# A planner that holds large transfers back while others fill the DMA queue, with q and k loaded per pair of heads and a new order table

## The chip, the cores and the metric

The program runs on one core of a Trainium2 chip, in one launch. The metric is device time in microseconds, the median of several runs. TensorE (PE, its weight loads PEld) multiplies; VectorE (DVE), ScalarE (ACT) and GpSimd (POOL) do the rest; SyncE (SP) only issues DMAs, all of them here, in a single queue that it works through in order.

## The reference, cut to what matters

Three stages follow each other, all in float32. (1) Attention: 4 batches, 12 heads, 448 rows, head width 64; q and k are normalized by their root mean square and scaled by a gain, then softmax(q k^T / 8) v. (2) A mixture of 4 causal attention experts on the 768-wide result: each row's two best experts, by `x @ w_gate`, are added with softmax weights. (3) A causal 5-tap convolution over rows makes a sigmoid gate, which multiplies `x @ w_val`; the product goes through `w_out`.

```
q_n, k_n = rmsnorm(q, g_q), rmsnorm(k, g_k)
x   = softmax(q_n k_n^T / 8) v                      # 4 x 12 heads
x   = sum over the 2 chosen experts e of  w_e * (softmax_causal(x wq_e (x wk_e)^T / 8) x wv_e) wo_e
out = (sigmoid(conv5(x)) * (x w_val)) w_out
```

## The kernel before, in words

Attention works on 24 pairs of heads (`pair`, n = 0 to 23). `normed` runs for every second pair: it loads q and k of four heads into one of two `raw` buffers (tiles w; lines 588 to 596), squares them on ACT (L601), sums on DVE (L605), gets the root by Ln and Exp (L614, L615) and a few small DVE steps (L619), and scales q and k into tiles s (L631, on POOL, on DVE for the first two pairs). For the first two pairs alone the load is already cut per pair, into one buffer each. `pair` then transposes on PE (L669), splits each value into a high and a low fp32r part (tiles qd, ql, xa), and needs copies of some halves on other partitions: those are small DMAs of 112 KB from on-chip memory to on-chip memory, two in `duplicate` (L559, L560) and two in `interleave` (L572, L573), where the second waits until the first has landed. They gate the score matmuls (L731). Row maximum (DVE L735), exp (ACT L736), transposes (PE L754), splits (L336, L759), and the products with v (L763, L765) follow; `row_factors` sends the reciprocal row sums through memory (L528, L530). Every sixth pair, `project` multiplies a finished batch with the expert weights (L789, L792). After the last pair the experts (`experts`, L958 to L1016), the fused output weights and the gate (`gated`, L1050 to L1085) and the output product (`project_out`, L1107, stores at L1116 to L1120) follow, batch by batch. `out_weights` brings `w_out` in twelve blocks through one buffer, rawb: load (L468), decoding on DVE (L474 to L476, L482), store (L853), reload (L855), split (L336, L331).

The order of the instructions of every engine is not written by hand. Each step is recorded by `op` with an engine, a planned duration, a priority vt (smaller is earlier; from the table `VT` and the step's place in its loop), a planned latency lat, and for a large DMA xfer, the time it occupies the DMA queue in the plan. `Plan.order` then plays the steps through: whenever an engine is free, it takes, of the steps whose inputs and buffers are there, the one of smallest vt, and so writes the order of each engine. `passed` is the planned time at which the DMA queue has emptied; a transfer begun now adds to it (line 231: `passed = max(now + ISSUE, passed) + pick.xfer`, ISSUE 500 ns) and is planned to land accordingly later. The chip has only the order: each engine runs its list in order, and an instruction waits there for what it needs.

On SP the priorities are, from first to last, in the table before: q and k loads (vt -1273 and on, `(n0 - VT["nl"]) * 12.6`), the gain loads `load_g` (-1247; four DMAs, planned as one step of 2500 ns without xfer), the row factors (-394 and on), `w_val` blocks, the on-chip copies (1421 and on), expert weights (2480 and on), v (7128 and on), and stores of the projections last.

Of the kernel before, what the change touches and what calls it, by code (L numbers as in the profile page):

```python
# [22 lines left out]


ISSUE = 500

# [22 lines left out]
def c_ptt(n):  # L49
# [8 lines left out]


VT = {  # L60
# [8 lines left out]
    "d_ph": 12.553, "d_pl": 32.0444, "d_ux": 525.5817, "d_ua": 647.7012, "d_um": 427.5213, "d_dup": 643.6909, "d_sc": 35.8393, "d_vh": 0.568, "d_vl":  # L69
    0.0, "d_kh": 122.0232, "d_ah": 141.9673, "d_xh": 355.494, "d_xl": 194.8804, "d_pv": 84.2769, "d_x2": 449.3647, "d_out": 580.9012, "d_oh":  # L70
    176.1229, "d_ol": 508.4987, "d_wh": 101.5984, "d_wl": 352.2573, "d_th": 19.0436, "d_tl": 137.7431, "d_v2h": 1061.6258, "d_v2l": 218.3702, "d_fh":
    674.3617, "d_fl": 711.8051, "d_qh": 577.4214, "d_ql": 60.1478, "d_evh": 721.7186, "d_evl": 349.74, "d_eah": 74.7536, "d_eal": 780.7673, "d_yh":
    629.5812, "d_yl": 391.7836, "d_gh": 461.9232, "d_tiny": 7.3052, "d_gl": 759.8279,
}


# [33 lines left out]
class Plan:  # L110
# [53 lines left out]
    def order(self):  # L164
        engs = ("pe", "act", "dve", "pool", "sp", "host")
        free_at = dict.fromkeys(engs, 0.0)
        queue = {e: [] for e in engs}
        events = []
        done = []

        def push(o):
            for x in o.alts:
                heapq.heappush(queue[x[0]], (o.vt, o.seq, o, x))
                if x[3] > 0.0:
                    heapq.heappush(events, (o.ready + 1000.0 * x[3], 2, o.seq, o))

        for o in self.ops:
            if o.npred == 0:
                push(o)
        now, ports, passed = 0.0, 0.0, 0.0  # L180
        left = len(self.ops)

        def can(o):
            need = {}
            for b in o.bufs:
                if b.kind is not None and b.phys is None:
                    g = self.groups[b.group]
                    if not b.kind.open or b.seq != g[2] + need.get(b.group, 0) or g[3] + need.get(b.group, 0) >= g[0]:
                        return False
                    need[b.group] = need.get(b.group, 0) + 1  # L190
                    need[b.kind] = need.get(b.kind, 0) + 1
                    if need[b.kind] > len(b.kind.free):
                        return False
            return True

        while left:
            progress = True
            while progress:
                progress = False
                for e in engs:  # L200
                    if free_at[e] > now:
                        continue
                    skipped, pick, choice = [], None, None
                    while queue[e]:
                        item = heapq.heappop(queue[e])
                        if item[2].begun:
                            continue
                        held = ports > now and item[2].port.get(e, False)
                        if not held and item[2].ready + 1000.0 * item[3][3] <= now and can(item[2]):
                            pick, choice = item[2], item[3]  # L210
                            break
                        skipped.append(item)
                    for item in skipped:
                        heapq.heappush(queue[e], item)
                    if pick is None:
                        continue
                    for b in pick.bufs:
                        if b.kind is not None and b.phys is None:
                            g = self.groups[b.group]
                            b.phys = b.kind.free.pop(0)  # L220
                            g[2] += 1
                            g[3] += 1
                    pick.begun = True
                    pick.eng, pick.dur, pick.fn, _ = choice
                    if pick.lat is None:
                        pick.lat = LAT[pick.eng]
                    free_at[e] = now + pick.dur
                    if pick.port.get(e, False):
                        ports = free_at[e]
                    if pick.xfer:  # L230
                        passed = max(now + ISSUE, passed) + pick.xfer
                        pick.lat += max(passed - free_at[e], 0.0)
                    pick.end = now + pick.dur
                    heapq.heappush(events, (pick.end, 0, pick.seq, pick))
                    heapq.heappush(events, (pick.end + pick.lat, 1, pick.seq, pick))
                    done.append(pick)
                    left -= 1
                    progress = True
            if not events:
                stuck = [(o.vt, o.eng, [(b.group, b.seq) for b in o.bufs if b.kind and b.phys is None]) for e in engs for _, _, o, _ in queue[e]]  # L240
                raise RuntimeError(f"the plan is stuck with {left} operations: {sorted(stuck)[:20]}")
            now = events[0][0]
            while events and events[0][0] <= now:
                _, what, _, o = heapq.heappop(events)
                if what == 2:
                    continue

                for s in o.succ:
                    if (len(s.alts) == 1 and s.eng == o.eng and o.eng in ("pe", "act")) == (what == 0):
                        s.npred -= 1  # L250
                        if s.npred == 0:
                            s.ready = now
                            push(s)
                if what == 0:
                    continue
                for b in o.bufs:
                    b.uses -= 1
                    if b.uses == 0 and b.kind is not None:
                        b.kind.free.append(b.phys)
                        self.groups[b.group][3] -= 1  # L260
                if o.eng == "host":
                    for kind in o.opens:
                        kind.open = True
        self.makespan = now
        return done
# [3 lines left out]
def tile_attn_moe_gate(  # L269
# [17 lines left out]
    nc = tc.nc  # L287
# [5 lines left out]
    T = 112  # L293
    NT = S // T
# [13 lines left out]
    op, buf = plan.op, plan.buf  # L308
# [50 lines left out]
    cw = cpool.tile([P, NCH, KC], F32, name="cw")  # L359
# [144 lines left out]
    TP = 12.6  # L504
# [70 lines left out]
    def normed(n0):  # L575

        b, p = divmod(n0, NPAIR)
        sqs = []
        for m0, nm in ((0, 1), (1, 1)) if n0 == 0 else ((0, 2),):
# [5 lines left out]
            def halves(raw=raw, nm=nm):  # L585
                return raw.t[0:T, 0 : 1024 * nm].rearrange("p (i m s t d) -> p i m s t d", i=2, m=nm, s=2, t=NT)

            for i, src in enumerate((q, k)):

                def load(i=i, src=src, raw=raw, m0=m0, nm=nm):  # L590
                    o = raw.t[0:T, 0 : 1024 * nm].rearrange("p (i h e) -> p i h e", i=2, h=2 * nm)[:, i]
                    h = 2 * (p + m0)
                    nc.sync.dma_start(o, src[b, h : h + 2 * nm].rearrange("h (p t) d -> p h (t d)", t=NT))

                op("sp", 450, load, (n0 - VT["nl"]) * TP - 2.0 * (n0 == 0), w=[raw], lat=1700, xfer=900 * nm)
            for m in range(nm):
                sq = buf(kS, "sq", QUOTA["sq"])
                sqs.append(sq)
# [17 lines left out]
            t = buf(kM, "t", 2)  # L616
# [551 lines left out]
```

## Time and profile before

| | us |
|---|---|
| median of 3 runs (642.06 to 643.44) | 642.58 |
| the profiled execution's own time | 643.4 |
| its span, first to last instruction | 641.6 |
| PE busy | 591.3 (92%) |
| PEld busy | 540.5 (84%) |
| DVE busy | 517.7 (81%) |
| ACT busy | 476.1 (74%) |
| POOL busy | 395.9 (62%) |

Of the span 1.8 us lie outside the profile's first and last instruction (643.4 less 641.6), and the profiled execution is 0.8 us above the median of the runs. Busy time is what an engine's instructions cover; DMA-issuing instructions are not counted. The clock column is the granted TensorE clock as a share of its full level (2.4 GHz; the lower level is 1.2 GHz); its mean over the span is 0.987.

### The profile page before, as it was taken

How to read it: one execution, taken by the hardware profiler on the slowest of the kernel's cores; microseconds unless marked ns; L12 is line 12 of the kernel's file. 1: busy time of each engine (PE TensorE's matmuls, PEld its weight loads, DVE VectorE, ACT ScalarE, POOL GpSimd, SP SyncE). 2: the span in 40 equal slices, each digit the busy share in tenths (PEclk: the TensorE clock that was granted, in tenths of full speed). 3: DMA queues.
4: the chain of work that ended last, by engine and by line, in shares of the span. 5: the costliest groups of instructions: out<-in, count | busy, mean ns of one | idle time of the engine just before them, and what ended most of it. 6: DMA issues, size and time to landing. Idle time of an engine off the chain costs nothing.

```text
span 641.6 us, 11699 instructions
## 1 busy us (share of the span) xinstructions
PE 591.3 (92%) x3626; PEld 540.5 (84%) x3626; DVE 517.7 (81%) x1013; ACT 476.1 (74%) x1189; POOL 395.9 (62%) x568
## 2 busy tenths in 40 slices
PE   1697799999999999999999999999869999999997
PEld 0575689888988988988989899989669999999997
DVE  5899899899999989999998938899987765973800
ACT  4798788789988988989886747777795677583431
POOL 4469775676758685958572467788887296216050
PEclk9899999999999999999999999999879999999999
DMA  6627751584273753543335387747343233100111
GB/s 172 139 49 165 147 129 42 154 191 144 56 179 90 181 138 100 145 128 101 90 96 170 105 252 221 207 156 240 107 135 116 75 93 89 39 26 32 46 49 64
DMA packets 70658, 77.93 MB, mean 121 GB/s; under 512 B 23442, under 2 KB 66618, under 8 KB 70596
## 3 DMA queue, kind: packets, MB, share of 16 engines
q1 hardware_dynamic: 70596, 77.18, 44.3%
q8 instruction: 29, 0.48, 0.3%
q14 instruction: 33, 0.27, 0.1%
HBM read 47.52 MB, written 15.87 MB: 99 GB/s over the span
## 4 chain that ended last, share of the span: by engine, by line
PE 53%; DVE 19%; DMA 10%; ACT 9%; POOL 4%; issue 3%; SPq 1%; ACTq 0%; DVEq 0%; POOLq 0%
PE bank L1107 12%; PE bank L789 6%; PE bank L731 6%; PE bank L754 6%; DVE x L759 4%; PE bank L1077 3%; PE bank L763 3%; DMA qd<-qd 3%; PE bank L792 3%; DVE m L735 3%; PE bank L1050 3%; ACT f L736 2%; PE bank L765 2%; ACT x L336 2%; PE bank L1008 2%
## 5 line engine op out<-in xcount | busy, mean ns | idle before, releaser
L336 ACT ACTIVATE x<-bank 128x448 fp32r<-128x448 f32 (+6 forms) x260 | 122.9, 505 | 21.5 <-PE bank L1008 10.4
L736 ACT ACTIVATE f<-bank,m 128x448 f32<-128x448 f32 x168 | 106.3, 633 | 23.4 <-DVE m L735 19.9
L759 DVE TENSOR_TENSOR x<-bank,x 128x448 fp32r<-128x448 f32 x192 | 114.9, 615 | 7.1 <-ACT x L336 4.6
L754 PE MATMUL bank<-ident,f 128*128 128x128 f32 (+1 forms) x768 | 111.6, 279 | 6.1 <-ACT f L736 5.8
L754 PEld LDWEIGHTS bank<-ident,f 128*128 128x128 f32 (+1 forms) x768 | 101.2, 176 | 15.7 <-ACT f L736 7.0
L735 DVE TENSOR_REDUCE m<-bank 128x1 f32<-128x448 f32 x168 | 103.0, 614 | 6.1 <-PE bank L731 5.0
L763 PE MATMUL bank<-x,ra 128*128 128x448 f32 x192 | 78.3, 409 | 5.5 <-DVE x L759 3.9
L731 PE MATMUL bank<-xa,qd 128*128 128x448 f32 x192 | 72.1, 396 | 11.6 <-DVE xa L697 5.5
L1107 PE MATMUL bank<-wp,rb 128*128 128x384 f32 x308 | 73.0, 341 | 0.3 <-POOL rb L331 0.3
L789 PE MATMUL bank<-x,wp 128*128 128x448 f32 x288 | 72.7, 378 | 0.0
L1058 DVE SCALAR_TENSOR_TENSOR f<-bank,cw,f 128x445 f32<-128x445 f32 (+3 forms) x96 | 59.5, 673 | 9.4 <-ACT f L1054 9.1
L731 PE MATMUL bank<-xa,ql 128*128 128x448 f32 x168 | 62.9, 375 | 0.0
L331 POOL TENSOR_TENSOR f<-f,f 128x448 f32<-128x448 f32 x32 | 37.3, 1166 | 30.6 <-DVE f L540 8.7
L631 POOL TENSOR_TENSOR s<-w,m 112x512 f32<-112x512 f32 x46 | 48.2, 1071 | 12.7 <-DVE m L619 11.0
L765 PE MATMUL bank<-x,ra 128*128 128x448 f32 x144 | 54.5, 379 | 1.3 <-DVE x L759 1.2
L1107 PEld LDWEIGHTS bank<-wp,rb 128*128 128x128 f32 x308 | 54.6, 188 | 1.1 <-POOL rb L331 0.6
L789 PEld LDWEIGHTS bank<-x,wp 128*128 128x128 f32 x288 | 50.9, 189 | 3.5 <-ACT f L736 0.2
L731 PEld LDWEIGHTS bank<-xa,qd 128*128 128x128 f32 x192 | 36.7, 194 | 17.1 <-POOL ra L331 5.8
L1107 PE MATMUL bank<-wp,ra 128*128 128x384 f32 x196 | 50.9, 343 | 0.0
L540 DVE TENSOR_TENSOR f<-bank,f 64x448 f32<-64x448 f32 x64 | 39.6, 619 | 10.9 <-ACT f L336 8.9
L763 PEld LDWEIGHTS bank<-x,ra 128*128 128x128 f32 x192 | 36.5, 190 | 13.3 <-DVE x L759 8.4
L792 PE MATMUL bank<-wp,x 128*112 128x260 f32 x288 | 44.4, 291 | 0.0
(170 smaller groups left out, 1426.1 us busy)
## 6 DMA issues: line engine op xcount, KB each, us to landing
f<-rr_d SPq DMA_DIRECT2D x64, 112.0 KB
xa<-xa SPq DMA_DIRECT2D x59, 112.0 KB
qd<-qd SPq DMA_DIRECT2D x46, 112.0 KB
w<-in_q_dram SPq DMA_DIRECT2D x11, 448.0 KB
w<-in_k_dram SPq DMA_DIRECT2D x11, 448.0 KB
s<-in_v_dram SPq DMA_DIRECT2D x12, 384.0 KB
s<-in_moe_w_val_dram SPq DMA_DIRECT2D x12, 384.0 KB
rawb<-in_moe_w_out_dram SPq DMA_DIRECT2D x12, 384.0 KB
```

What stands on the lines that cost most here:

```text
L336: either(kinds, dvt, n, act=lambda: nc.scalar.activation(out(), a(), AF.Copy), vec=lambda e: e.tensor_scalar(out(), f32(a()), 1.0, 1.0, op ...
L731: nc.tensor.matmul(sc.t[:, 0:S], l, r, start=(m == 0), stop=(m == len(ops) - 1))
L735: op("dve", c_dve(S), lambda i=i, sc=sc: nc.vector.tensor_reduce(nm.t[:, i : i + 1], sc.t[:, 0:S], axis=AX.X, op=ALU.max, negate=True), vt ...
L736: op("act", c_act(S, 2), lambda i=i, sc=sc: nc.scalar.activation(a[i].t, sc.t[:, 0:S], AF.Exp, bias=nm.t[:, i : i + 1], accum_out=sm.t[:, ...
L754: nc.tensor.transpose(at.t[0:cn, P * i : P * (i + 1)], a[3 * s + i].t[:, cols], ident)
L759: op("dve", c_dve(S), lambda at=at, hi=hi, lo=lo, cn=cn, r0=r0, own=own: nc.vector.tensor_tensor(lo.t[r0 : r0 + cn], at.t[0:cn, own], hi.t ...
L763: nc.tensor.matmul(acc.t[:, 0:S], l, hi.t, start=(j == 0), stop=(j == 3))
L765: nc.tensor.matmul(acc.t[:, 0:S], l, lo.t, start=False, stop=False)
L789: nc.tensor.matmul(acc.t[:, 0:S], wp[:, w, c, m * P : (m + 1) * P], x.t, start=first, stop=last)
L792: nc.tensor.matmul(acc.t[0:T, 0:VC], x.t[:, t * T : (t + 1) * T], wp[:, w, c, 2 * ED : WC], start=first, stop=last)
L1058: nc.vector.scalar_tensor_tensor(gc.t[:, d:S], acc.t[:, 0 : S - d], cw[:, c, KC - 1 - d : KC - d], gc.t[:, d:S], op0=ALU.mult, op1=ALU.add)
L1107: nc.tensor.matmul(acc.t[:, 0:NH], l.t[:, cols], wout[:, w, c, NH * h : NH * (h + 1)], start=(c == 0 and i == 0), stop=(c == NCH - 1 and i ...
```

## The change

A transfer of xfer 600 or more is not begun by the plan while the planned queue reaches more than 1000 ns ahead of now; when it has drained to that point, an event lets SP look again. The loads of q and k are cut into one per pair of heads and tensor (224 KB, xfer 1050) also for the blocks after the first. And all priorities have new values. The rest of the kernel, its buffers and its arithmetic are as before.

```diff
+HOLD, BIG = 1000, 600
 VT = {
-    "pw": 197.4989, "nl": 101.0747, ...  "vl": -565.7674, "tr": -112.8122, ... "lg": -1246.9721, ...
+    "pw": 223.8855, "nl": 297.1005, ...  "vl": -797.0996, "tr": -109.5638, ... "lg": -1785.5091, ...
     ...
-                        held = ports > now and item[2].port.get(e, False)
+                        held = ports > now and item[2].port.get(e, False) or item[2].xfer >= BIG and passed > now + HOLD
     ...
                     if pick.xfer:
                         passed = max(now + ISSUE, passed) + pick.xfer
                         pick.lat += max(passed - free_at[e], 0.0)
+                        heapq.heappush(events, (passed - HOLD, 2, pick.seq, pick))
     ...
-            for i, src in enumerate((q, k)):
-                def load(i=i, src=src, raw=raw, m0=m0, nm=nm):
-                    o = raw.t[0:T, 0 : 1024 * nm].rearrange("p (i h e) -> p i h e", i=2, h=2 * nm)[:, i]
-                    h = 2 * (p + m0)
-                    nc.sync.dma_start(o, src[b, h : h + 2 * nm].rearrange("h (p t) d -> p h (t d)", t=NT))
-                op("sp", 450, load, (n0 - VT["nl"]) * TP - 2.0 * (n0 == 0), w=[raw], lat=1700, xfer=900 * nm)
+            for m in range(nm):
+                for i, src in enumerate((q, k)):
+                    def load(i=i, src=src, raw=raw, m0=m0, nm=nm, m=m):
+                        o = raw.t[0:T, 0 : 1024 * nm].rearrange("p (i h e) -> p i h e", i=2, h=2 * nm)[:, i, 2 * m : 2 * m + 2]
+                        h = 2 * (p + m0 + m)
+                        nc.sync.dma_start(o, src[b, h : h + 2].rearrange("h (p t) d -> p h (t d)", t=NT))
+                    op("sp", 450, load, (n0 - VT["nl"]) * TP - 2.0 * (n0 == 0), w=[raw], lat=1700, xfer=1050)
```

In the new table the order of the classes on SP is the same: q and k (-3743 and on), the gain loads (-1785), row factors (-881 and on), the first `w_val` block, the on-chip copies (1380 and on), expert weights (2813 and on), v (10043 and on).

## Rows read from the trace of the kernel before

**Rows 1.** Windows: span in stages; busy of each engine, clock, DMA share, GB/s.
```profile
core 0: us, PE busy (x) PEld busy (x) DVE busy (x) ACT busy (x) POOL busy (x), PEclk, DMA share, GB/s
0.00:10.00 10.00, 0.00 (x0) 0.00 (x0) 3.80 (x10) 4.83 (x8) 3.90 (x23) 1.00 0.62 164
40.00:85.00 45.00, 37.00 (x208) 29.91 (x209) 39.04 (x68) 37.19 (x90) 38.95 (x51) 0.96 0.58 124
100.00:340.00 240.00, 232.70 (x1490) 210.81 (x1490) 226.80 (x421) 210.34 (x521) 166.46 (x232) 1.00 0.47 124
450.00:480.00 30.00, 22.24 (x116) 19.45 (x115) 25.36 (x58) 23.78 (x61) 24.39 (x34) 0.83 0.43 123
500.00:641.60 141.60, 137.57 (x821) 132.32 (x820) 74.72 (x161) 75.85 (x186) 51.39 (x82) 1.00 0.18 55
```

**Rows 2.** Waits of PE over the whole span: us in total, times, longest.
```profile
PE bank L669 <- DVE m L619: 10.5, 1, 10.5
PE bank L1008 <- DVE f L1085: 4.8, 1, 4.8
...
PE bank L731 <- DMA qd<-qd: 2.7, 3, 1.8
...
PE bank L731 <- DMA xa<-xa: 1.2, 2, 0.7
```

**Rows 3.** Chain that ended last, between 55 and 79 us: start, us, what.
```profile
55.82 7.53 DMA qd<-qd
...
63.44 2.12 DMA qd<-qd
...
70.31 6.31 DMA qd<-qd
76.70 2.17 DMA qd<-qd
```

**Rows 4.** SP's issues: copies behind q and k loads, and one without.
```profile
54.23 0.43 SPq L593 DMA_DIRECT2D w<-in_q_dram  x1
54.76 0.43 SPq L593 DMA_DIRECT2D w<-in_k_dram  x1
...
55.82 0.48 SPq L559 DMA_DIRECT2D qd<-qd  x1
...
63.44 0.48 SPq L560 DMA_DIRECT2D qd<-qd  x1
...
330.58 0.48 SPq L559 DMA_DIRECT2D qd<-qd  x1
...
333.11 0.47 SPq L560 DMA_DIRECT2D qd<-qd  x1
```

**Rows 5.** Waits of SP's queue over the whole span: us in total, times, longest.
```profile
SPq L560 <- DMA qd<-qd: 34.6, 13, 4.8
```

**Rows 6.** Timeline of the start: issues of SP and the first steps behind them.
```profile
1.17 0.45 SPq L593 DMA_DIRECT2D w<-in_k_dram  x1
2.66 0.58 SPq L447 DMA_DIRECT2D g<-in_g_q_dram  x1
4.55 0.60 SPq L448 DMA_DIRECT2D g<-in_g_k_dram  x1
4.62 1.06 ACT L601 ACTIVATE s<-w 112x1024 f32<-112x1024 f32 x1 [2.62 <-DMA w<-in_k_dram]
7.46 0.21 DVE L452 TENSOR_SCALAR gg<-g 128x1 f32<-128x1 f32 x1 [0.53 <-DMA g<-in_g_k_dram]
7.69 1.22 DVE L605 TENSOR_REDUCE m<-s 112x16 f32<-112x1024 f32 x1
8.83 0.88 DVE L619 SCALAR_TENSOR_TENSOR m<-m,m 112x16 f32<-112x16 f32 x4
```

**Rows 7.** Windows within the start of attention, same columns as rows 1.
```profile
55.00:60.00 5.00, 3.04 (x19) 2.18 (x17) 5.00 (x9) 4.44 (x12) 4.66 (x7) 1.00 0.98 219
75.00:80.00 5.00, 2.78 (x11) 2.00 (x12) 2.94 (x6) 3.65 (x10) 4.42 (x6) 0.90 0.79 146
80.00:85.00 5.00, 5.00 (x26) 4.45 (x25) 4.34 (x7) 3.82 (x10) 4.75 (x7) 0.76 0.33 76
```

**Rows 8.** Who waits for the q and k loads, over the whole span.
```profile
  DMA w<-in_k_dram: 4.9, 4
```

**Rows 9.** SP's issues of rawb: the last four of twelve loads.
```profile
441.13 0.38 SPq L468 DMA_DIRECT2D rawb<-in_moe_w_out_dram  x1
463.42 0.33 SPq L468 DMA_DIRECT2D rawb<-in_moe_w_out_dram  x1
469.76 0.37 SPq L468 DMA_DIRECT2D rawb<-in_moe_w_out_dram  x1
481.70 0.34 SPq L468 DMA_DIRECT2D rawb<-in_moe_w_out_dram  x1
```

More of the change, by code (lines that the diff above doesn't have):

```diff
@@ L60 @@
 VT = {
[8 rows of a table removed]
[L69 to L73, printed above, removed]
[8 rows of a table added]
+    "d_ph": 67.3095, "d_pl": 232.558, "d_ux": 559.7588, "d_ua": 561.4908, "d_um": 271.0272, "d_dup": 479.8107, "d_sc": 20.7623, "d_vh": 1.0708,
+    "d_vl": 0.0, "d_kh": 120.8591, "d_ah": 376.0376, "d_xh": 412.9286, "d_xl": 84.9786, "d_pv": 128.2464, "d_x2": 670.1971, "d_out": 188.3538, "d_oh":
+    354.9454, "d_ol": 340.6525, "d_wh": 26.7103, "d_wl": 274.7178, "d_th": 187.244, "d_tl": 187.6038, "d_v2h": 1073.4642, "d_v2l": 843.0787, "d_fh":
+    834.5908, "d_fl": 830.1554, "d_qh": 690.35, "d_ql": 157.8726, "d_evh": 759.1297, "d_evl": 398.9279, "d_eah": 557.6893, "d_eal": 1050.2794, "d_yh":
+    115.3421, "d_yl": 268.7796, "d_gh": 210.8442, "d_tiny": 4.6612, "d_gl": 816.7842,
 }
```

16 rows, old and new, of the table VT are left out of this document.

## The prediction

> **What bounds the kernel now.** I read the stage windows first, then the waits of PE, then the chain, and last SP's issues. In the windows [rows 1] the reader is to see three kinds of stretches. From 500 us to the end PE is busy 137.57 of 141.6 us: that stretch is PE's, and no transfer can give it much. From 100 to 340 us PE is busy 232.7 of 240 (3.0% idle) and DVE 226.8 (5.5% idle): two engines are nearly full. The room lies in three places: the start, where PE waits 10.5 us for its first input [rows 2]; 40 to 85 us, where PE idles 8.0 of 45 us and DVE 6.0; and 450 to 480 us, where PE idles 7.8 of 30 and the clock that it is granted is 0.83 [rows 1].
>
> PE's waits on the small on-chip copies, the transfers that the new rule is to let through, are 2.7 + 1.2 = 3.9 us in all [rows 2]. The chain says more than that sum: between 55.8 and 79 us it runs over these copies for 7.53 + 2.12 + 6.31 + 2.17 = 18.1 us [rows 3]. SP's issues show why [rows 4]. At 54.23 and 54.76 it issues 448 KB of q and of k, right behind them the first copy at 55.82, and the second, which waits until the first has landed, goes out at 63.44: 7.6 us later. Where no such load is ahead, the same step takes 2.5 us (330.58 to 333.11). So a block's loads cost a copy about 5.1 us. SP, which works in order, stood 34.6 us in 13 such waits [rows 5], yet PE waited for it only 3 times. In most blocks the delay is hidden behind work on other pairs.
>
> **The change: the start, +1.1 us.** The new rule can be played through in the code for the first steps. The plan's times (ns) only give an order here. At 0 SP takes the first q load; `passed` becomes 500 + 1050 = 1550. At 450 SP is free, and k is next by priority, but 1550 > 450 + 1000, so it is held, by 100 ns. The gain loads have no xfer, cannot be held and come next in priority: one step of four DMAs, 2500 ns. So the first k goes out fifth from there, not second, and k of the second pair after two more small transfers. On the chip a gain issue takes 0.58 to 0.60 us [rows 6]; four of them with the gaps are from 2.66 to 4.55 + 0.60, that is 2.5 us. The first k is issued at 1.17 and lets the square begin at 4.62 [rows 6]; I expect its issue near 3.7 and the square near 7.0 (a little less than 2.5 later, since fewer bytes are in the queue). Two things are given back: the wait of DVE for the gains, 0.53 us, goes, since they land earlier; and the sum of the second pair (7.69, 1.22 us) no longer stands in front of the first pair's small steps, which begin at 8.83 and could have begun about 0.8 earlier [rows 6]. So 2.4 - 0.5 - 0.8 = +1.1. Bounds: -0.5, if the square is no later and only the gain wait goes, and +2.5, if nothing is given back. PE has no other work then, and DVE is busy from there on, so all of it reaches the end.
>
> **The copies, -4.6 us.** Between 40 and 85 us a copy that finds at most one load of 224 KB ahead should take some 3 us rather than 7.6. PE's direct waits there and the clock that falls behind the longest one (0.90 and 0.76 in 75 to 85 us [rows 7]) would give 2.8 us of the 3.9 and 0.1 x 2.8 + 0.24 x 5.0 = 1.5 us. But DVE sets how much can be had: it idles 6.0 us of the 45, and at the 5.5% of the following stretch it would idle 2.5. In 55 to 60 us it is busy all 5.0 us while the copy is outstanding [rows 7]. So I take the excess, 3.5 us. In the rest of attention the direct waits left are 3.9 - 2.8 = 1.1 us, and I take them all: -4.6 in sum. Bounds: 0 (DVE's list fills the time anyway) and -8.0, all of PE's idle time in the 45 us.
>
> **The split of q and k, 0.** 22 loads of 448 KB become 44 of 224 KB, 22 issues more of some 0.47 us [rows 4], 10.3 us of SP in 300. Cover: loads run a block ahead into the second raw buffer, and in the whole span only 4 squares waited for one, 4.9 us, most of it at the start [rows 6, 8]. If that cover is gone, the price is in the fourth rival. What is queued behind a load that waits for its raw buffer is every later transfer on SP, copies too; the four loads of a block wait for the same buffer, so this head is not longer than before.
>
> The Trainium skill speaks against the split: "DMA: Bandwidth & Descriptors", section Rules for kernel authors, asks for one large transfer in place of many small ones. The windows lean its way so far: 164 GB/s at the start, where q and k come in loads of 224 KB [rows 1], against 219 GB/s where they are 448 KB [rows 7]; but other small transfers lie in both.
>
> **The new table, 0.** The order of the classes on SP is unchanged (read from the diff), so the rule and the split decide what changes there. What else moves in the lists can't be read from rows. The place with most at stake is 450 to 480 us. There PE idles 7.8 us, 4.8 of it in one wait [rows 2], and at clock 0.83 the 22.2 busy us hold 3.8 us of loss: 11.5 us at most to gain. `w_out` passes through one buffer in twelve loads, the last four at 441, 463, 470 and 482 us [rows 9], and the output product cannot finish a tile before the last. Each load is now subject to the rule, and so is each store behind it. I take 0, with -11.5 on one side; on the other, if a pair of copies that waits 2.8 us on SP (2.5 and a little [rows 4]) stands ahead of each of four loads, +11.2.
>
> **Sum.** +1.1 - 4.6 = -3.5 on the execution's 643.4: 639.9, its span 638.1. The median of the runs lies 0.8 below this execution, so 639.1.
>
> **Rivals.**
> (1) The `w_out` chain is pulled in: with others held, its loads find an emptier queue, and the idle stretch shrinks by some 60% of 11.5 us: 639.1 - 7 = 632. For it: a hole of 22 us between two loads of rawb [rows 9]. Against: DVE, which decodes each block, is busy 25.4 of those 30 us [rows 1].
> (2) The copies were hidden anyway: the DVE bound takes all of it, 642.6 + 1.1 - 1.1 = 642.6. For it: DVE 5.0 of 5.0 us [rows 7], and only 3 waits of PE. Against: the 2 us in which DVE too stood still from 75 to 80 us.
> (3) Slower: the `w_out` chain is pushed back. Small transfers that wait for their source now stand on SP ahead of large ones that could run. Three of the last four rawb loads each 2.8 us later: 639.1 + 8.4 = 647.5. It decides from 4.8 us on (643.9). For it: one buffer, no run-ahead, PE dry there already. Against: SP's priorities are as before.
> (4) The start costs more and the copies give nothing: 642.6 + 2.5, and pair 1 behind by as much again until its k lands: 645 to 647, say 645.5.
> (5) Small loads are slower loads: 896 KB of a block at 164 GB/s rather than 219 take 5.6 rather than 4.2 us; if the four blocks up to about 135 us, where the square has little lead, pay it: 639.1 + 5.6 = 644.7. For it: a square waited for k 4 times [rows 8]. Against: later blocks have a whole block of lead. This is what the rule cited above would do here.
>
> **How the numbers follow.** A difference under 0.2% (1.3 us) can't be told from none. The forecast (636 to 642) has 0.46, of which 0.04 lies above 641.3; rival (1) 0.12, (2) 0.12, (3) 0.15, (4) 0.09, (5) 0.06. Faster: 0.42 + 0.12 + 0.02 of (2) = 0.56. Same: 0.04 + 0.08 of (2) + 0.02 of (4) and (5) = 0.14. Slower: 0.02 + 0.15 + 0.13 = 0.30. The range: from 630, past the value of (1) but short of its bound, to 649, past that of (3): some 0.08 lies outside on either side, mostly lists that the new table turns over in ways no row shows.
>
> **What would show it.** The start: gain issues directly behind the first q, the first square near 7 us, PE's first matmul near 11.5 rather than 10.5. The copies: the second of a pair issued at most 4 us behind the first also where q and k are near; PE's waits on copies under 1 us; a clock of 1.00 from 75 to 85 us; DVE idle near 2.5 us in 40 to 85. The split: squares waiting under 6 us for loads in all. The table: 450 to 480 us, or where the same work then lies, with some 22 us of PE busy at a clock near 0.83. The prediction is wrong if the stretch from 500 us on, counted from the last rawb load, is longer, if attention's end moves by more than 5 us in either direction, or if copies still lie behind large loads.

## The result, and the profile after

The changed kernel takes 651.66 us, the median of 4 runs (651.39 to 652.22); the kernel before takes 643.01 beside it. The ratio is 1.0128 [1.0094, 1.0162]: 8.6 us slower, where 3.5 us faster was forecast. The profiled execution took 651.39, its span is 649.5, the granted clock 0.984 (0.987 before). The lines of the file stand 4 or 5 higher than before (L593 is L598, L619 is L624, L631 is L636, L669 is L674, L560 is L564, L468 is L472).

The stage windows of the kernel after, in the columns of [rows 1]:

```profile
0.00:10.00 10.00, 0.00 (x0) 0.00 (x0) 1.69 (x4) 2.65 (x3) 3.89 (x23) 1.00 0.51 129
40.00:85.00 45.00, 40.73 (x240) 33.71 (x238) 41.71 (x77) 40.63 (x100) 31.29 (x43) 0.99 0.49 127
100.00:340.00 240.00, 231.66 (x1481) 208.98 (x1478) 229.78 (x424) 210.32 (x526) 161.71 (x224) 1.00 0.49 132
366.00:420.00 54.00, 51.63 (x341) 48.55 (x339) 29.19 (x76) 33.83 (x98) 36.35 (x45) 1.00 0.69 209
450.00:480.00 30.00, 23.42 (x115) 18.63 (x114) 27.23 (x66) 22.04 (x56) 19.48 (x26) 0.86 0.48 135
500.00:641.60 141.60, 141.29 (x837) 135.71 (x836) 79.84 (x169) 77.27 (x187) 57.77 (x102) 1.00 0.18 57
```

From 40 to 85 us PE is busy 40.73 instead of 37.00 us, and the clock no longer falls; that is what the change was forecast to give. From 366 to 420 us DVE is busy only 29.19 us. Before, the same window had 37.95:

```profile
366.00:420.00 54.00, 53.46 (x356) 50.27 (x355) 37.95 (x92) 35.07 (x104) 38.14 (x47) 1.00 0.75 228
```

The start, on SP, ACT and DVE in turn (timeline of the kernel after; it answers to [rows 6]):

```profile
0.72 0.39 SPq L598 DMA_DIRECT2D w<-in_q_dram  x1
1.17 0.58 SPq L451 DMA_DIRECT2D g<-in_g_q_dram  x1
...
3.71 0.59 SPq L598 DMA_DIRECT2D w<-in_k_dram  x1
...
5.31 0.66 SPq L657 DMA_DIRECT2D s<-in_v_dram  x1
6.01 0.60 SPq L598 DMA_DIRECT2D w<-in_k_dram  x1
```
```profile
6.50 1.06 ACT L606 ACTIVATE s<-w 112x1024 f32<-112x1024 f32 x1 [4.50 <-DMA w<-in_k_dram]
8.91 0.31 ACT L619 ACTIVATE m<-m,eps 112x16 f32<-112x16 f32 x1 [1.35 <-DVE m L610]
10.07 1.06 ACT L606 ACTIVATE s<-w 112x1024 f32<-112x1024 f32 x1 [0.86 <-DMA w<-in_k_dram]
11.04 0.20 ACT L620 ACTIVATE m<-m 112x16 f32<-112x16 f32 x1
```
```profile
11.16 1.22 DVE L610 TENSOR_REDUCE m<-s 112x16 f32<-112x1024 f32 x1 [2.35 <-ACT s L606]
12.30 0.58 DVE L624 SCALAR_TENSOR_TENSOR m<-m,m 112x16 f32<-112x16 f32 x3
14.06 1.51 DVE L624 SCALAR_TENSOR_TENSOR m<-m,m 112x16 f32<-112x16 f32 x1 [1.18 <-ACT m L620]
15.49 0.28 DVE L340 TENSOR_SCALAR ra<-s 128x256 fp32r<-128x256 f32 x1
...
16.20 1.08 DVE L335 TENSOR_TENSOR ra<-s,ra 128x256 fp32r<-128x256 f32 x3
17.21 1.28 DVE L636 TENSOR_TENSOR s<-w,m 112x512 f32<-112x512 f32 x2
```

SP does what the forecast said, to the slot: first q, four gain loads, then k at 3.71; the first square starts at 6.50 (about 7.0 was forecast). What follows is new. On ACT the square of the second pair stands ahead of the first pair's second small step (L620); it waits for its own k until 10.07, so that step runs at 11.04. On DVE the sum and small steps of pair 1 and the splitting of v (`ra<-s`) stand ahead of the first pair's scaling, L636, which begins at 17.21. PE's first wait, 10.5 us in [rows 2], becomes:

```profile
PE bank L674 <- DVE s L636: 18.0, 1, 18.0
```

SP's waits at the second copy of a set, answering to [rows 5], and the squares' waits for loads, answering to [rows 8]:

```profile
SPq L564 <- DMA qd<-qd: 14.8, 11, 3.3
```
```profile
  DMA w<-in_k_dram: 5.4, 2
```

And the last four of the twelve loads of rawb, answering to [rows 9], 6 to 17 us later each:

```profile
457.98 0.34 SPq L472 DMA_DIRECT2D rawb<-in_moe_w_out_dram  x1
470.27 0.53 SPq L472 DMA_DIRECT2D rawb<-in_moe_w_out_dram  x1
477.99 0.33 SPq L472 DMA_DIRECT2D rawb<-in_moe_w_out_dram  x1
487.47 0.34 SPq L472 DMA_DIRECT2D rawb<-in_moe_w_out_dram  x1
```

To see where time is lost and made up I use one curve below. Every matmul of a shape is given the same length, these are summed in the order in which PE ran them, and two kernels are compared at the time at which each had done the same work (us of work; all of it is some 565). After minus before:

```
work        0.1   20   40   60  100  200  300  350  370  390  410  500
after      +7.6 +9.7 +0.7  0.0 +2.8 +2.7 +3.3 +4.4 +5.1 +8.3 +9.6 +8.1
```

So the start costs 7.6 to 9.7 us, the stretch to 102 us (work 60) gives all of that back, some 4 us are lost again through the attention (to work 350), 2.8 of them before work 100, and some 5 more between there and 490 us (work 410). The experiments take these pieces one at a time.

Two cautions. Other lengths for the shapes move the curve's values by about 1 us. And it compares one trace of each kernel: that of the kernel before has a granted clock of 0.987 and 643.4 us, while beside the experiments the same kernel took 645 to 647 us. So the curves of s2, s8b, s10b and s12 below end 2 to 3.5 us higher than their ratios say. What counts in them is where they rise; what a piece is worth is taken from the ratios.

### The profile page after: what moved, and what is told of

Its sections match the earlier page's. It is cut to its first block, busy times and chain, and to the rows that moved or that the text cites. A ratio compares the mean times of both kernels' runs of the same rounds, so it can differ in the third digit from the quotient of the medians.

```text
span 649.5 us, 11717 instructions
## 1 busy us (share of the span) xinstructions
PE 594.9 (92%) x3626; PEld 542.1 (83%) x3626; DVE 512.0 (79%) x1019; ACT 475.4 (73%) x1196; POOL 386.2 (59%) x556
## 4 chain that ended last, share of the span: by engine, by line
PE 38%; DVE 6%; DMA 6%; ACT 3%; issue 1%; POOL 1%; SPq 0%; ACTq 0%; POOLq 0%; DVEq 0%
PE bank L1112 13%; PE bank L1082 4%; PE bank L1055 3%; PE bank L794 3%; PE bank L759 3%; PE bank L736 2%; DVE f L1063 2%; PE bank L1013 1%; DMA rawb<-in_moe_w_out_dram 1%; PE bank L768 1%; PE bank L998 1%; DVE x L335 1%; DMA r_v<-rv_d 1%; PE bank L1021 1%; PE bank L999 1%; PE bank L770 1%
## 5 line engine op out<-in xcount | busy, mean ns | idle before, releaser
L340 ACT ACTIVATE x<-bank 128x448 fp32r<-128x448 f32 (+6 forms) x260 | 121.3, 502 | 24.4 <-PE bank L1013 11.8
L741 ACT ACTIVATE f<-bank,m 128x448 f32<-128x448 f32 x168 | 105.9, 631 | 15.3 <-DVE m L740 10.5
L759 PEld LDWEIGHTS bank<-ident,f 128*128 128x128 f32 (+1 forms) x768 | 102.7, 176 | 14.4 <-ACT f L741 6.6
L636 POOL TENSOR_TENSOR s<-w,m 112x512 f32<-112x512 f32 x46 | 50.4, 1111 | 28.8 <-DVE m L624 18.9
L340 ACT ACTIVATE f<-bank 64x448 f32<-64x448 f32 x64 | 34.5, 539 | 17.6 <-PE bank L768 8.8
L768 PEld LDWEIGHTS bank<-x,ra 128*128 128x128 f32 x192 | 36.7, 191 | 11.2 <-DVE x L764 7.3
L736 PEld LDWEIGHTS bank<-xa,qd 128*128 128x128 f32 x192 | 36.5, 194 | 11.2 <-issue 3.8
```

Of the source, the lines that this page charges most:

```text
L340: either(kinds, dvt, n, act=lambda: nc.scalar.activation(out(), a(), AF.Copy), vec=lambda e: e.tensor_scalar(out(), f32(a()), 1.0, 1.0, op ...
L636: eng.tensor_tensor(o, halves()[:, i, m], f, ALU.mult)
L736: nc.tensor.matmul(sc.t[:, 0:S], l, r, start=(m == 0), stop=(m == len(ops) - 1))
L741: op("act", c_act(S, 2), lambda i=i, sc=sc: nc.scalar.activation(a[i].t, sc.t[:, 0:S], AF.Exp, bias=nm.t[:, i : i + 1], accum_out=sm.t[:, ...
L759: nc.tensor.transpose(at.t[0:cn, P * i : P * (i + 1)], a[3 * s + i].t[:, cols], ident)
L768: nc.tensor.matmul(acc.t[:, 0:S], l, hi.t, start=(j == 0), stop=(j == 3))
```

## The experiments

All ratios are to the kernel before, run beside each kernel; 0.1% is 0.64 us.

Ranges in brackets are 95% intervals.

**The start.** Two kernels rearrange the first steps of the planned list, with nothing else changed:

```diff
-    for o in plan.order():
+    done = plan.order()
+    LEAD = [...]          # s1: 13 entries, s2: 75
+    done[: len(LEAD)] = [done[i] for i in LEAD]
+    for o in done:
```

s1_loads_first puts the loads of pairs 0 and 1 ahead of the gain loads.

> The changed kernel, with four of SP's first steps moved: the first q and k loads of pairs 0 and 1 stand in front of the gain loads again, as in the kernel before; nothing else is moved on any engine. Theory A (the start is what the change costs: PE's first matmul at 18.0 instead of 10.5 us, and nothing gives it back): the square begins near 4.7 us, PE's first matmul comes some 2 us earlier (about 16), and the median falls by as much, to about 649.5 from 651.7. Theory B (the start was made up by 100 us, where both kernels have done the same PE work at 102.2 us, and the loss lies in the new order behind that): PE begins about 2 us earlier too, but the median stays within 1 us of 651.7.

Measured: 1.0172 [1.0103, 1.0241]. The loads alone repair nothing; the wait has moved by 0.7 us:

```profile
PE bank L674 <- DVE s L636: 17.3, 1, 17.3
```

s2_start_as_before puts the steps of the first two pairs in the old order on every engine's list.

> The changed kernel, with the steps of the first two pairs in the order of the kernel before, on SP, ACT, DVE and POOL: loads of pairs 0 and 1 first, the scaling of pair 0 right behind its small steps, the splits of v and of the first expert weights behind them; from the score matmuls of pair 0 on, the order is untouched. Theory A (the start is what the change costs): PE's first matmul near 10.5 to 11.5 us, and the median near 645, about 7 below the changed kernel. Theory B (the start is made up anyway, the loss lies behind 100 us): the same early matmul, but the lead is lost again by 100 us and the median stays within 1.5 of 651.7.

Measured: 1.0057 [1.0027, 1.0087]. PE's first matmul is back at 10.3 us, and the start is worth 1.0128 - 1.0057 = 0.71%, 4.6 us. The curve stands at -4.1 at work 40 (76.8 us against 80.8) and still ends at +7.1, the ratio at +3.7 us: there is a second loss behind.

**The parts alone.** e_tableonly is the kernel before with the new table; e_ruleonly is the kernel before with the rule (and its event), so old table and loads of 448 KB. No kernel has the split alone.

```diff
-VT = {...}                                 # before
+VT = {...}                                 # e_tableonly: the new one
-held = ports > now and ...
+held = ports > now and ... or item[2].xfer >= BIG and passed > now + HOLD   # e_ruleonly
```

> The kernel before with the new table alone: no rule, q and k in loads of 448 KB. If the new table is by itself a good order (theory C: the rule or the split costs the time), it comes out near 643 or below. If table and rule only fit each other (theory D), it is slower than the changed kernel, over 655.

> The kernel before with the rule alone: old table, q and k in loads of 448 KB. Theory C (the rule costs the time by what it does on SP): near 652. Theory D (any change of the plan's rules under a table made for others upsets the lists of all engines): far more, over 660.

Measured, in two runs each: 1.0239 [1.0178, 1.03] and 1.0712 [1.0628, 1.0795]. Both are as theory D has them: neither part stands without the other. The table alone loses nothing to the end of the attention (curve 0.0 at work 340) and then some 16 us by work 400. Its windows, and behind them the same of the kernel before:

```profile
340.00:420.00 80.00, 77.15 (x509) 71.81 (x508) 56.75 (x123) 54.77 (x149) 46.21 (x61) 1.00 0.52 157
420.00:500.00 80.00, 62.89 (x352) 54.81 (x351) 69.37 (x154) 58.15 (x162) 57.38 (x77) 0.87 0.51 147
```
```profile
340.00:420.00 80.00, 79.26 (x511) 73.47 (x510) 61.95 (x137) 55.34 (x155) 48.69 (x59) 1.00 0.64 195
420.00:500.00 80.00, 71.10 (x426) 65.39 (x425) 70.06 (x150) 58.54 (x154) 64.99 (x97) 0.94 0.48 147
```

The rule alone loses 23 us by work 100 and goes on losing in the attention, where PE idles 17.4 us of 240.

**Gathered loads, whole kernel.** s6_gathered has the loads of one buffer at the place of the first:

```diff
+        if o.fn.__name__ == "load":
...
+            n = place.setdefault(key, [i, 0])
+            place[id(o)] = n[0] + 0.1 * n[1]
...
+    done.sort(key=lambda o: place[id(o)])
```

> The changed kernel with its planned order, except that the q and k loads of one buffer (four from pair 2 on) are issued by SP one behind the other at the place of the first, as in the kernel before, instead of being spaced out by the planner with copies between them. 35 of the 48 loads move forward on SP; ACT, DVE, POOL and PE keep their orders. Theory E (the spacing of the loads on SP made up the lost start): the copies again queue behind four loads; SP's waits at the copies (14.8 us in the changed kernel, 34.6 before) go back above 25 us, PE's waits on xa or xs between 40 and 100 us come back, the work-lag curve against the kernel before, which fell from +9.7 us at work 20 to 0.0 at work 60, stays at +4 us or more at work 60, and the time is 654 to 660. Theory F (the new table's order on the other engines made it up, by planning the copies earlier against their readers): the curve still falls to within 2 us of zero at work 60, PE's waits there stay under 2 us, and the time is 650 to 653.

Measured: 1.018 [1.0143, 1.0217], 0.52% or 3.3 us above the changed kernel, but the two intervals overlap. The trace gives theory E half of its signs: the curve stands near +5 at work 60, where the changed kernel's is back at 0, but SP's waits at the second copy rise only from 14.8 to 18.9 us (over 25 was expected), and PE waits for no copy between 40 and 100 us:

```profile
SPq L564 <- DMA qd<-qd: 18.9, 12, 3.9
```

So the spacing seems to give back time, and not by the waits that theory E named; s12 below asks again in a faster kernel.

**The chain of w_out.** s7_chain_early lets blocks 2 to 12 take the places of blocks 1 to 11; s7_start_and_chain has the start of s2 as well.

```diff
+    SHIFT = {2678: 2604.01, ...}     # op number: new place, 92 of them
+    PHYS = {('outt', 1): 3, ...}     # tiles handed out anew, 43
+    done = [done[i] for i in sorted(range(len(done)), key=lambda i: SHIFT.get(i, i))]
...
+            x.phys = PHYS.get((x.group, x.seq), x.phys)
```

> The changed kernel, with the preparation of w_out's twelve blocks (load, splits, gate multiply, transposes, evictions, their reload) begun one block earlier: blocks 2 to 12 take the places in the order that blocks 1 to 11 had; nothing else is moved. Theory G (the second loss, after 366 us, is the chain of w_out pushed back: the order gives block 2 its load 9.5 us after its buffer was free, and every later block follows it): the last two loads, at 477.99 and 487.47 us in the changed kernel, come 6 to 9 us earlier, the granted clock of 460 to 500 us rises above 0.93, and the time falls by 3 to 5 us, to 647 to 649. Theory H (the loss lies in the order of the other work of the output stage, or in SP's copies there, and the chain only follows it): the loads come earlier by less than 3 us or the time stays within 1.5 us of 651.7.

> The changed kernel with both repairs: the steps of the first two pairs in the order of the kernel before (as in s2_start_as_before, ratio 1.0057 to before) and w_out's preparation one block earlier (as in s7_chain_early). Theory G: the two losses add up and both go; 649.9 less 3 to 5 us less what s2's own chain had lost, a ratio to before of 0.996 to 1.001, that is 641 to 644 on a chip where before takes 643: the four microseconds that the copies gave are then seen at the end. Theory H: the ratio stays at 1.004 to 1.007.

Measured: 1.0139 [1.0111, 1.0166] and 1.0093 [1.0065, 1.0121]. The chain did move. In s7_chain_early the second load of rawb went out at 377.35 us after 387.06, and the last two were 3.7 and 5.4 us earlier than in the changed kernel:

```profile
482.03 0.33 SPq L472 DMA_DIRECT2D rawb<-in_moe_w_out_dram  x1
```

The clock from 480 to 500 us was lower all the same, 0.76 against 0.87 in the changed kernel, and the time did not fall. Theory G fails: an earlier chain by itself gives nothing. Since 43 tiles had to be handed out anew for it, and s8 below shows that this can cost time of its own, it doesn't show that the chain is harmless. The pair repeats the worth of the start: 1.0139 - 1.0093 = 0.46%, 3.0 us here after 4.6 above.

**Orders written out.** The next kernels replace the planner's result by a list: numbers of operations, the engine where there is a choice, and in the later ones the tile.

```diff
+    def follow(self, order, choice, take):
+        for i in order:
...
+            o.eng, o.dur, o.fn, _ = o.alts[choice.get(i, 0)]
...
+                    b.phys = b.kind.free.pop(n.pop(0) if n else 0)
...
-    for o in plan.order():
+    for o in plan.follow(ORDER, CHOICE, TAKE):
```

> The order is written out by hand here, the planner is not used: the start of the kernel before (as in s2_start_as_before), the attention in the order of the changed kernel, and from w_out's preparation on (about 366 us) the operations of the output stage in the order, and on the engines, that the kernel before gave them. Its rule and its split loads are those of the changed kernel. Since moving w_out's chain alone gave nothing (ratio 1.0139 after 1.0128, and 1.0093 after 1.0057), theory G is weakened; this run asks for the whole stage. Theory H (the second loss lies in the new order of the output stage as a whole): s2_start_as_before, 1.0057, loses its last 5 to 7 us, ratio 0.996 to 1.001; the work-lag curve stays within 2 us of zero from work 340 on. Theory I (the loss comes from what the attention hands over: the state of the buffers and queues at 366 us, or the boundary itself): the curve rises between work 340 and 410 again and the ratio stays at 1.004 or more.

> The reverse: the kernel before to the end of its attention, by an order written out, and the output stage in the order and on the engines of the changed kernel. Theory H: the lag is zero to 366 us and then grows to 5 to 7 us; ratio 1.007 to 1.012. Theory I: ratio within 1.003.

> An order written out: the start of the kernel before, then the changed kernel's order for what it plans in its first 95 us (the copies with the loads spaced out between them), and everything later in the order of the kernel before, loads of a pair of pairs behind one another. If the spaced loads gave back what the lag curve says (s2_start_as_before is 4 us ahead of before at work 40) and the rest is as before, the curve stays at -3 to -5 us to the end: ratio 0.992 to 0.996, the fastest of all. If the gain is lost again at the next stage that has a bound of its own (DVE at 95% busy from 100 us on), the curve goes back to zero by work 100 to 300 and the ratio is 0.999 to 1.003.

Measured: 1.0096 [1.0058, 1.0134], 1.0188 [1.0144, 1.0231], 1.0062 [1.0025, 1.0098]. These three had no TAKE: each tile went to the first in the order in which the list frees them. ACT's timeline of s8 shows what that costs:

```profile
437.92 0.39 ACT L505 ACTIVATE r_v<-bank 112x260 f32<-112x260 f32 x1 [0.18 <-PE bank L962]
441.13 0.58 ACT L505 ACTIVATE qd<-f 128x448 fp32r<-128x448 f32 x1 [2.82 <-DMA xa<-qd]
```

The tile just freed in the list is still read by a copy on the chip, and ACT stands 2.82 us in front of it. So the three decide nothing, though s9, the reverse of s8, is slow where theory H has it: its curve rises by 9 us between work 350 and 410. Two were built again with the free tile whose last use is planned to end first:

> s8_old_output_stage once more with one flaw of that kernel taken out. Its list handed out tiles in the order in which the program frees them; in its trace ACT stands 2.82 us at 437.9 us because the tile that it writes (qd) is still read by a copy that has just been issued, where the kernel before writes xa at that place and does not wait, and PE then waits 3.1 us for ACT. Here the free tile whose last use is planned to end first is taken, as the planner does. Theory H (the second loss lies in the new order of the output stage): the curve stays within 2.5 us of zero from work 340 on, ratio 0.997 to 1.002. Theory I (it comes with what the attention hands over, whatever the order after it): the curve still rises by 4 us or more between work 370 and 410 and the ratio stays at 1.005 or more.

> s10_first_95 once more with the tiles handed out in the same way and the change-over put at 80 us of the plan, where fewer operations change their places; the curve of s10_first_95 stood at -4.1 us at work 60 and at +3.2 at work 80, so it lost at the change-over what the copies had given. If the gain of the spaced loads lasts: -3 to -5 us from work 40 to the end, ratio 0.992 to 0.997, faster than before. If it is given back in the attention, whose DVE is busy 95 of 100 us from there on: zero by work 300, ratio 0.999 to 1.003.

Measured: s8b 0.9982 [0.9957, 1.0008], s10b 0.9932 [0.9902, 0.9963]. Theory H holds: s2 and s8b run the same list on ACT, DVE, POOL and PE to 380 us, and the old order of the output stage takes the ratio from 1.0057 to 0.9982, 0.75% or 4.8 us. Their lists differ in one place ahead of that: in s8b three loads of later pairs stand in front of a v load on SP and go out near 12.5 rather than 17.2 us. In the curve that puts s8b 1 to 2 us ahead through most of the attention, but only 0.2 us at work 350, so nearly all of the 4.8 us are the output stage's. The window of s2 and then of s8b:

```profile
366.00:420.00 54.00, 50.31 (x334) 47.18 (x333) 30.54 (x77) 34.34 (x102) 38.14 (x47) 1.00 0.70 209
```
```profile
366.00:420.00 54.00, 52.08 (x344) 48.21 (x343) 38.12 (x89) 34.78 (x105) 39.55 (x49) 1.00 0.76 234
```

DVE does 7.6 us more of its work before 420 us, as in the kernel before (37.95). The second load of rawb goes out at 374.93 rather than 383.02 us. In the curve the loss between work 350 and 410, 7.0 in s2, is 3.1 in s8b. What is left arises where the clock of s8b is lower than in the kernel before, 0.73 against 0.83 in 450 to 480 us:

```profile
450.00:480.00 30.00, 23.36 (x102) 20.04 (x101) 23.48 (x54) 22.18 (x56) 22.31 (x33) 0.73 0.37 111
```

s10b goes on: only the first 80 us of the plan are new, the rest is the old order. It beats the kernel before by 0.68% (641.78 us beside 647.06), the fastest of all here. Its distance to s8b, 0.50% or 3.2 us, is what the new order of the attention costs behind 80 us; the two intervals overlap by a little, so this term is the least sure. Only some 2.5 us of it are there in the curve at the attention's end (work 340); the rest comes in the output stage, where both have the old order but s10b a clock of 0.83 and s8b one of 0.73.

**The spacing by itself.** s12_gathered_80 is s10b with a single thing undone on SP: 11 entries of ORDER move forward (the twelfth that is counted below stood in its place already), so that the loads of the first 80 us stand four in a row.

> s10b_first_80 with one thing undone: in its first 80 us the four q and k loads of a pair of pairs are issued by SP one behind the other, at the place of the first; 12 loads move forward on SP, and ACT, DVE, POOL and PE keep their orders and tiles. Theory E (the spacing made up the time): the copies again queue behind the loads, SP's wait between copies of one set in 30 to 100 us comes up from next to nothing to some 8 to 10 us as in the kernel before (10.2 us), the curve, at -4.1 us at work 40 in s10b_first_80, comes to -1 or above, and the ratio goes from 0.9932 to 0.998 to 1.003. Theory F (the order of the copies and their readers in the new table made it up): SP's waits come back, but the readers have room; the curve stays within 1.5 us of s10b_first_80 and the ratio is 0.991 to 0.996.

Measured: 1.0025 [1.0001, 1.0049]. Theory E holds: the spacing is worth 1.0025 - 0.9932 = 0.93%, 6.0 us, the curve at work 60 goes from -2.2 to +3.3. But not by the copies' waits alone. SP's issues in s12, and then pieces of its chain in 33 to 105 us (start, us, what):

```profile
37.05 0.54 SPq L778 DMA_DIRECT2D w<-in_q_dram  x1
...
38.70 0.40 SPq L778 DMA_DIRECT2D w<-in_k_dram  x1
39.15 0.45 SPq L697 DMA_DIRECT2D s<-in_moe_w_gate_dram  x1
39.78 0.50 SPq L744 DMA_DIRECT2D qd<-qd  x1
```
```profile
39.15 4.93 DMA s<-in_moe_w_gate_dram
44.10 0.85 ACT wp L520
...
75.31 3.51 DMA rr_d<-f
...
79.39 2.78 DMA f<-rr_d
82.34 1.16 POOL f L515
```

Behind four loads the small gate weights take 4.93 us to land, and a row of sums takes 3.51 us to DRAM and 2.78 back; both lie on the chain, and ahead of the row it runs through SP's four issues themselves, 72.90 to 75.21. In s10b the gate weights are issued behind one load, at 37.35, and between 40 and 74 us its chain runs over ACT, DVE and PE alone. There the same row goes out behind one load and is read back 2.6 us after its issue; a later one, with no load of q or k issued in the 8 us ahead of it, after 1.2 us:

```profile
70.15 0.79 SPq L778 DMA_DIRECT2D w<-in_q_dram  x1
70.99 0.37 SPq L712 DMA_DIRECT2D rr_d<-f  x1
...
73.61 1.11 SPq L714 DMA_DIRECT2D f<-rr_d  x2
...
83.44 0.28 SPq L712 DMA_DIRECT2D rr_d<-f  x1
84.65 1.10 SPq L714 DMA_DIRECT2D f<-rr_d  x2
```

The waits on copies that theory E named did not come back to 8 us; what came back is that other small transfers, gate weights and row sums, are late. How the 6.0 us divide between them was not tried; up to 1.8 us of it may be the clock, which is 0.91 in s12 and 1.00 in s10b from 80 to 100 us (0.09 x 20).

## Why the prediction was wrong, point by point

Two steps failed. The new table was put at 0, and the new order that comes of it costs some 4.8 us in the output stage and some 3 in the attention. The start was put at +1.1 us and is worth 3.0 to 4.6. The third term, the copies, was about right.

- **The new table, 0: the step that failed most.** "The order of the classes on SP is unchanged, so the rule and the split decide what changes there" left out that the table orders ACT, DVE and POOL too. And on SP it holds only for the classes of the attention. Worked out from the two tables (`T1` is the planned start of the output stage, other for each table), the third load of rawb had priority T1 - 250, ahead of the second batch's expert loads (T1 - 233) and copies (T1 + 29); with the new table it has T1 + 121, behind both (T1 - 492 and T1 - 345). The traces show such a turn at the second load (whether by the table or by the rule isn't shown): before, it goes out ahead of three of the first batch's copies that stand at 379.13, 381.39 and 382.43; after, behind all of them:

```profile
378.17 0.39 SPq L468 DMA_DIRECT2D rawb<-in_moe_w_out_dram  x1
```
```profile
385.38 0.47 SPq L564 DMA_DIRECT2D xa<-xa  x1
...
387.06 0.38 SPq L472 DMA_DIRECT2D rawb<-in_moe_w_out_dram  x1
```

  What the runs show in place of 0: 4.8 us in the output stage (s8b against s2) and some 3.2 in the attention (s10b against s8b). These are orders that table and rule made together; that the table has a share in the first is shown by e_tableonly, which loses there without the rule. The bound on that side, +11.2, held it; the value did not.
- **The start, +1.1 us: failed.** The issues on SP came as said. One step that failed is the 0.8 us given back: the sum of pair 1 still stands in front of the first pair's small steps (11.16 before 12.30), and because it waits for its own late load it now holds them longer. I had followed the transfer and what stands behind it for one pair. In lists that are worked through in order, a late operation of another pair (the square that waits for its k) and early ones (v's splits; v's small transfers pass under the rule) stand in front as well: first matmul +7.6. The other is "PE has no other work then, and DVE is busy from there on, so all of it reaches the end": of 7.6 us, 4.6 do (s2).
- **The copies, -4.6 us: right in kind and about in size.** The clock from 75 to 85 us stays at 1.00, as said, PE's waits on copies at the score matmuls fall from 3.9 to 0.5 us, and DVE idles 3.3 of the 45 us (2.5 were said):

```profile
75.00:80.00 5.00, 5.00 (x33) 4.47 (x32) 4.87 (x11) 4.51 (x14) 3.02 (x4) 1.00 0.63 177
80.00:85.00 5.00, 4.97 (x28) 4.05 (x27) 4.77 (x9) 4.52 (x11) 3.17 (x5) 1.00 0.45 125
```

  Taking the spacing back costs 3.3 us in the whole kernel (s6, not clear of noise) and 6.0 in s10b (s12). The mechanism was too narrow: the sum counted PE's waits on copies only, not the row sums and gate weights in the same queue. And the 5.1 us that [rows 4] were read for are not q's and k's alone: a load of v, 384 KB, went out between them and the copy, at 55.30.
- **The split, 0: not shown.** No run has it alone. The squares waited 5.4 us for loads, under the 6 said, in two waits at the very start. The rule of the Trainium skill ("DMA: Bandwidth & Descriptors", Rules for kernel authors) asks for one large transfer in place of many small ones. Rival (5), which took small loads to be slower, needs squares that wait for later loads, and none does. The windows that were read for it, 164 and 219 GB/s, compare little: the DMA share was 0.62 in one and 0.98 in the other.
- **The sum:** 4.6 + 4.8 + 3.2 - 6.0 = +6.6 us, and s12 leaves 1.6 for what the new order of the first 80 us costs with the loads gathered: +8.2 us, 1.28%. It comes out by construction, since the terms are the steps of one row of kernels (the changed one, s2, s8b, s10b, s12, the one before), so it is a division of the loss and no check of it. Each term is a difference of two ratios that are known to some 0.3%, so within 2 us or so.
- **The rivals.** (3) named the stretch and was nearest, 647.5, with 0.15. Its place was right, rawb's last loads did go out late, and what spoke against it, "SP's priorities are as before", was false there. Its mechanism was not shown: the chain moved alone (s7) gave nothing, the order of the whole stage did. (4) had half of the start's cost, and the copies did give something.
- **The signs.** Of those that were to show the prediction wrong, one came: from the last rawb load to the end it is 162.0 us, 159.9 before. PE's first matmul came at 18.0, not near 11.5.

Open stays which of the output stage's operations matters most. That DVE's work comes late there is seen; that a particular one does it wasn't tried.

## What to carry to other kernels

When a long transfer has short ones behind it in the same queue, count every short transfer whose reader is near, not only the ones that a wait list names, and spread the long ones: here that alone gave 0.9% (s12 against s10b). When a planner's rule or its table changes, read the new lists of all engines at the start and at each stage's border, for the cost of an early step lies in what else now stands in front of it. If a part of the new order is good, keep that part: the first 80 us of it with the old rest is the fastest kernel here.

## What was not expected

A tile that is free in the program's order need not be free on the chip: handing tiles out by that order rather than by the planned end of their last use is all that s8 and s8b differ in, 1.0096 against 0.9982, with 2.82 us of it seen in one wait of ACT.
